# Batch 0 of a cosine attention with a low-rank mixer: keys transposed unnormed, their norms in the scale of the exp

## The chip, the cores and the metric

One NeuronCore of a Trainium2 chip runs the whole program. The metric is the time of one execution in device microseconds (us). Its engines work side by side and wait for each other through semaphores: TensorE (PE in the profile), VectorE (DVE), ScalarE (ACT), GpSimd (POOL) and SyncE (SP), the last two used here mainly to issue transfers. Each engine takes its instructions in the order in which the program lists them.

## What is computed

For 8 batches, 12 heads, 448 positions and 64 dimensions, cosine attention and then a mixer whose weights all batches share (d_model 768, rank 32, hidden 3072):

```python
q_n = q / (norm(q) + 1e-06);  k_n = k / (norm(k) + 1e-06)
scores = q_n @ k_n.T / tau                     # tau = 0.1
attn = softmax(scores)
x = (attn @ v) as [batch, seq, heads * dim]
u = x + (x.T @ U @ V).T
out = u + relu(u @ w_ch1) @ w_ch2
```

The scores are cosines divided by tau, so the kernel leaves the maximum of the softmax out and divides by the sum of the exps after the product with v.

## The kernel before

**Data.** q, k, v and the weights come from HBM in float32 and are cast to bfloat16 by the transfers themselves, which GpSimd issues (`load_qk`, `load_v0`, `load_v`, `load_w1`, `load_w2`). U and V come through SyncE as float32 and are cast by ScalarE (`cast_u`, `cast_v`). A position of the sequence is stored as s = 4 * row + c, so a tile of q or k has 112 rows and, per head, 4 chunks c of 64 dimensions.

**Norms** (`stats`). For a group of two or four heads, q and k are squared (L434 on ScalarE, L436 on VectorE), summed over the dimensions (L440, VectorE), and the inverse norm comes from Ln and Exp on ScalarE (L445, L448), then an addition of epsilon and a reciprocal on VectorE (L451, L453). It lands in a tile `inv`.

**Normed heads** (`norm`, pairs of heads). Two multiplies for the keys (L477) and one for the queries (L474) fill a tile `xn` of twelve blocks of 128 columns. Blocks 0 to 7 are keys: the first four hold head 0 in columns 0 to 63, the others head 1 in columns 64 to 127, and the other halves are zeros set once (L705). Blocks 8 to 11 hold the queries of both heads beside each other. For batches 0 and 1, `flip` transposes the blocks on TensorE (L363) against an identity, eight key blocks into one PSUM tile and four query blocks into another, and copies them to `qkT` (L700 on ScalarE, L702 on VectorE). Later batches use the transposing transfer.

**Attention** (`attention`). Per pair of batch 0 eight score matmuls (L508) of 112 key rows against 448 queries contract over all 128 rows, of which one half is zero; ScalarE takes the exp of each (L512) with the scale 1/tau. Then 16 matmuls per head multiply with v (L526), the sum of the exps coming along as an extra column of ones, and VectorE divides (L533, L535). The `attn` tiles are two, the PSUM tiles of scores three, the `qk_nat` tiles of loaded q and k three.

**v of batch 0** (`load_v0`). It is loaded in the order of q and k in two transfers (L408) and copied by ScalarE or VectorE into a layout with two extra columns, both lying in the space that w2 takes later.

**Mixer** (`stage0`, `mlp`). The products with U (L559) and V (L587), the addition of x (L601, and L596, L598 where two batches meet), transposes of u, then per batch 24 groups of six up-projection matmuls (L649) with a relu each (L659, L661), and the down-projection (L670) with the addition of u (L679). Two batches share seven row tiles: the even batch takes three, the odd one four.

**What sets the order.** Nothing is scheduled by hand. Every operation is put into a `Plan` with an engine (or two to choose from), a cost, its dependencies, the buffers that it takes and frees, and a priority (a low number goes first). `Plan.run` plays the program through with these costs and writes each engine's instructions down in the order of their planned starts. The chip keeps that order on each engine, whatever the times turn out to be. TensorE has several streams in a fixed precedence: transposes of q and k, products with v, the mixer's first matmuls, scores, and last the projections. Transfers on GpSimd have a planned busy time on one shared line (0.5 us per head for each of q and k, and for v of batch 0) and a planned delay (2 us, for later batches 8 us).

Of the kernel before, what the change touches and what calls it, by code (L numbers as in the profile page):

```python
# [200 lines left out]
def kernel(  # L201
# [45 lines left out]
    def fixed_ring(tiles):  # L247
# [10 lines left out]
    r_ln = ring(2, [SCH, 2, G, SC], FP, "ln")  # L258
    r_inv = ring(3, [SCH, 2, G, SC], FP, "inv")
    r_qkT = ring(6, [128, 12, SCH], BF, "qkT")  # L260
# [5 lines left out]

    VN = H * SC * D
    r_w2 = Ring(1, lambda i: pool.tile([128, VN + H * SC * (D + 2)], BF, name="raw_v", tag="w2", bufs=1)
                if i == 0 else pool.tile([128, NC, C], BF, name="w2_sb", tag="w2", bufs=1))
# [4 lines left out]

    def v_raw():
        return raw.tile[0:SCH, 0:VN].rearrange("p (h e) -> p h e", h=H)

    def v_first():
        return raw.tile[0:SCH, VN:].rearrange("p (h c d) -> p h c d", h=H, c=SC)

# [14 lines left out]
    V_sb = const.tile([128, PAD + S + PAD], BF, name="V_sb")  # L295
    ident = const.tile([128, 128], BF, name="ident")
    w1_sb = const.tile([128, CC, F], BF, name="w1_sb")

# [14 lines left out]
    plan = Plan()  # L313
    pe_tp = plan.stream("PE")
    pe_av = plan.stream("PE")
    pe_a = plan.stream("PE")
# [37 lines left out]

    def flip(stream, ins, n, into, part, deps, acq, rel):

        tp = Slot(r_mm, 1)
        tp.own = True
        for z, x in enumerate(ins):
            def fn(z=z, x=x):  # L360
                if z == 0:
                    tp.tile = psum.tile([128, len(ins), n], BF, name="tp", tag="mm", bufs=3)
                nc.tensor.transpose(out=tp.tile[:, z, :], in_=x(), identity=ident[:n, :n])  # L363
            o = plan.add(Op("PE", 0.05, fn, deps=deps + [id_set] if z == 0 else (), acq=[tp] + acq,
                            rel=rel if z == len(ins) - 1 else []), stream)
        c = plan.add(Op("ACT/DVE", any_t(n * len(ins), 2), None, deps=[o], acq=acq, rel=[tp],
                        prio=0.2, fast=True))
        c.fn = lambda: copy_op(c, *part(into(), tp.tile))
        return c
# [4 lines left out]

    def load_qk(b, h0, h1):
        ld = Slot(r_ld, 3 * (h1 - h0) // 2)
        ops = [load(lambda i=i, src=src: nc.gpsimd.dma_start(  # L377
            out=ld.tile[:, i, 0:h1 - h0, :],
            in_=src[b, h0:h1].rearrange("h (s c) d -> s h (c d)", c=SC)),
            (h1 - h0) * 0.5, acq=[ld], late=2.0 if b == 0 else LATE) for i, src in enumerate((q, k))]  # L380
        return ld, ops

# [23 lines left out]
    def load_v0(h0, h1):  # L406

        o = load(lambda: nc.gpsimd.dma_start(  # L408
            out=v_raw()[:, h0:h1, :], in_=v[0, h0:h1].rearrange("h (s c) d -> s h (c d)", c=SC)),
            (h1 - h0) * 0.5, acq=[raw])  # L410
        c = plan.add(Op("ACT/DVE", any_t(256 * (h1 - h0), 2), None, deps=[o, v0_set], prio=0.35,
                        fast=True))
        c.fn = lambda: copy_op(c, v_first()[:, h0:h1, :, 0:D],
                               v_raw()[:, h0:h1, :].rearrange("p h (c d) -> p h c d", c=SC))
        for h in range(h0, h1):
            got[0, h, "v"] = [c]

    def stats(b, h0, h1, ld, ops):

        g = h1 - h0  # L420
        pr = 0.3 if b == 0 else 4
        ss, ln, nv, inv = Slot(r_ss, 1), Slot(r_ln, 1), Slot(r_ln, 1), Slot(r_inv, 3 * g // 2)
        red = []
        for i in range(2):
            for a0 in range(0, g, G // 2):
                a1 = min(g, a0 + G // 2)
                sq = Slot(r_sq, 1)
                o = Op("ACT/DVE" if b == 0 else "DVE", any_t(256 * (a1 - a0), 2, 0.17), None,
                       deps=[ops[i]], acq=[sq], prio=pr + 0.2, fast=True)

                def square(o=o, i=i, a0=a0, a1=a1, sq=sq):
                    x, y = ld.tile[:, i, a0:a1, :], sq.tile[:, 0:a1 - a0, :]
                    if o.by == "ACT":
                        nc.scalar.activation(out=y, in_=x, func=AF.Square)  # L434
                    else:
                        nc.vector.tensor_mul(y, x, x)  # L436
                o.fn = square
                plan.add(o)
                red.append(plan.add(Op("DVE", dve_t(256 * (a1 - a0)),
                    lambda i=i, a0=a0, a1=a1, sq=sq: nc.vector.reduce_sum(  # L440
                        ss.tile[:, i, a0:a1, :].rearrange("p h c -> p (h c)"),
                        sq.tile[:, 0:a1 - a0, :].rearrange("p h (c d) -> p (h c) d", d=D),
                        axis=AX.X),
                    deps=[o], acq=[ss], rel=[sq], prio=pr + 0.1)))
        o = plan.add(Op("ACT", 0.25, lambda: nc.scalar.activation(  # L445
            ln.tile[:, :, 0:g, :], ss.tile[:, :, 0:g, :], AF.Ln),
            deps=red, acq=[ln], rel=[ss], prio=0))
        o = plan.add(Op("ACT", 0.2, lambda: nc.scalar.activation(  # L448
            nv.tile[:, :, 0:g, :], ln.tile[:, :, 0:g, :], AF.Exp, scale=0.5),
            deps=[o], acq=[nv], rel=[ln], prio=0))  # L450
        o = plan.add(Op("DVE", 0.21, lambda: nc.vector.tensor_scalar_add(  # L451
            nv.tile[:, :, 0:g, :], nv.tile[:, :, 0:g, :], EPS), deps=[o], prio=pr))
        o = plan.add(Op("DVE", 0.35, lambda: nc.vector.reciprocal(  # L453
            inv.tile[:, :, 0:g, :], nv.tile[:, :, 0:g, :]), deps=[o], acq=[inv], rel=[nv], prio=pr))
        for p in range(h0 // 2, h1 // 2):
            norm(b, p, ld, inv, 2 * p - h0, [o], pr)

    count = [0]

    def norm(b, p, ld, inv, a, deps, pr):  # L460


        by_pe = b < PE_BATCHES
        xn, qkT = Slot(r_xn, 2 if by_pe else 1), Slot(r_qkT, 8 if b == 0 else 7)
        deps = deps + [xn_set[count[0] % len(xn_t)]]
# [30 lines left out]
    def attention(b, p, X):  # L496
        off = PAD * (b % 2)
        qkT, qdeps = got.pop((b, p, "qkT"))
        attn = Slot(r_attn, 2)
        exps = {}  # L500
        small = b == 0
        rows_ = SCH if small else 128
        for m in range(8 if small else 7):
            sc = Slot(r_sc, 1)

            def score(sc=sc, m=m):
                kT = qkT.tile[:, 0:8, :].rearrange("p b s -> p (b s)")
                nc.tensor.matmul(out=sc.tile[0:rows_, 0:S], lhsT=kT[:, rows_ * m:rows_ * (m + 1)],  # L508
                                 rhs=qkT.tile[:, 8:12, :].rearrange("p c s -> p (c s)"),
                                 start=True, stop=True)  # L510
            o = plan.add(Op("PE", pe_t(S), score, deps=qdeps, acq=[sc], rel=[qkT]), pe_sc)
            exps[m] = plan.add(Op("ACT", act_t(S), lambda sc=sc, m=m: nc.scalar.activation(  # L512
                out=attn.tile[0:rows_, m, off:off + S], in_=sc.tile[0:rows_, 0:S], func=AF.Exp,
                scale=inv_tau), deps=[o], acq=[attn], rel=[sc], prio=0.1 if b == 0 else 1))
        muls = []
# [182 lines left out]
    def copy_op(op, dst, src):  # L698
        if op.by == "ACT":
            nc.scalar.copy(out=dst, in_=src)  # L700
        else:
            nc.vector.tensor_copy(out=dst, in_=src)  # L702


    xn_set = [fill(lambda t_=t_: nc.vector.memset(t_[:, 0:8, :], 0.0), 1024, prio=i - 3)  # L705
              for i, t_ in enumerate(xn_t)]
# [19 lines left out]
    def load_u(par):  # L726
        off = PAD * par
        ops = []
        for t in range(4):
            lo, hi = max(0, 128 * t - off), min(S, 128 * (t + 1) - off)  # L730
            for n, c, s0, s1 in segments(lo, hi):
                r0 = n + off - 128 * t
                ops.append(plan.add(Op("SP", 0.45, lambda t=t, c=c, s0=s0, s1=s1, r0=r0: nc.sync.dma_start(  # L733
                    out=U_f()[r0:r0 + s1 - s0, par, t, :], in_=rows(moe_U, c, s0, s1)),
                    deps=[zf], prio=-2, lat=2.5)))
        return ops
# [4 lines left out]
    def cast_v():  # L741
        nc.scalar.copy(out=V_sb[:, PAD:PAD + S].rearrange("r (c s) -> r s c", c=SC),
                       in_=V_f().rearrange("r (s c) -> r s c", c=SC))

# [10 lines left out]
    def att(b):  # L755
        X = Slot(r_X, 0)
        muls = []
        for p in range(NPAIR):
            muls += attention(b, p, X)
        return stage0(b, X, muls)  # L760

    u0 = load_u(0)
    v0 = [plan.add(Op("SP", 0.45, lambda t=t: nc.sync.dma_start(out=V_f()[R * t:R * (t + 1)], in_=moe_V),  # L763
                      acq=[uv], prio=-2, lat=2.5)) for t in range(4)]
    u1 = load_u(1)
    first = load_qk(0, 0, 2)
    id_set = plan.add(Op("POOL", 0.5, lambda: make_identity(nc, ident)), pool_q)
    stats(0, 0, 2, *first)
    go(0, 2, 4)
    load_v0(0, 4)  # L770
    go(0, 4, 8)
    load_v0(4, 12)
    go(0, 8, 12)
    for i in range(NW):
        w1_ops.append(load_w1(i, NW))
    consts = [plan.add(Op("ACT", 0.25, lambda: cast_u(0), deps=u0 + [z], rel=[uv], prio=3)),
              plan.add(Op("ACT", 0.5, cast_v, deps=v0 + [z], rel=[uv], prio=3)),
              plan.add(Op("ACT", 0.25, lambda: cast_u(1), deps=u1 + [z], rel=[uv], prio=3))]
# [55 lines left out]
```

## Time and profile before

| what | us |
|---|---|
| median of the runs (3, 611.57 to 612.37) | 612.14 |
| the profiled execution's own time | 612.43 |
| span from its first to its last instruction | 610.5 |
| TensorE busy | 585.5 |
| VectorE busy | 298.6 |
| ScalarE busy | 285.0 |
| first score of batch 0 starts | 16.02 |
| first exp of batch 0 starts | 16.59 |
| last exp of batch 0 ends | 44.92 |
| first up-projection of batch 0 starts | 48.05 |
| first transposes of batch 1 start | 61.05 |
| first down-projection of batch 0 starts | 89.65 |

Times inside the execution count from the start of the span. Busy time counts an instruction from its start to its end; TensorE's matmuls are pipelined and their ends are modelled, so a busy TensorE is not one at its peak. A row of a timeline gives start, duration, engine, line, operation, output and input, and, in brackets, how long the engine stood idle before it and what it waited for. The chain of waits is followed back from the last instruction: at each step to what released it, or to the instruction before it on its engine.

### The profile page before, as it was taken

What the parts mean: (1) busy time and instruction counts of PE and PEld (TensorE: products, weight loads), DVE (VectorE), ACT (ScalarE), POOL (GpSimd) and SP (SyncE); (2) the same over time, 40 slices, a digit from 0 to 9 for tenths busy, and PEclk for the clock granted to TensorE, in tenths of its full rate; (3) what the DMA queues carried; (4) which work ended last, traced back from release to release, by engine and by line L of the source; (5) the groups of instructions that cost most, each with busy time, mean ns of one, the idle gap of its engine ahead of it and who ended that gap; (6) DMA issues with size and microseconds to landing.
All of it is one profiled execution on the core that took longest, in us unless ns stands there. A gap on an engine that the chain in (4) does not pass through costs nothing.

```text
span 610.5 us, 11561 instructions
## 1 busy us (share of the span) xinstructions
PE 585.5 (96%) x4704; PEld 348.3 (57%) x4728; DVE 298.6 (49%) x758; ACT 285.0 (47%) x609; POOL 109.9 (18%) x168
## 2 busy tenths in 40 slices
PE   0899999999999999999999999999999999999997
PEld 0565666555555665666445666666545666654465
DVE  6977859989999799654820253014300210110011
ACT  4984981288774187407642067505542015014300
POOL 6227160135340627000600000000000000000000
PEclk9999999999999999999999999999999999999999
DMA  9999992999999999644962132031002110410011
GB/s 136 202 204 136 210 156 23 166 138 138 132 125 155 139 185 159 94 84 83 121 37 53 53 72 59 1 84 35 14 1 52 52 40 1 79 52 1 0 53 53
DMA packets 146037, 54.58 MB, mean 89 GB/s; under 512 B 109568, under 2 KB 145984, under 8 KB 145984
## 3 DMA queue, kind: packets, MB, share of 16 engines
q0 software_dynamic: 69216, 25.96, 37.9%
q1 hardware_dynamic: 76704, 27.86, 24.5%
q8 instruction: 37, 0.61, 0.4%
q14 instruction: 16, 0.13, 0.1%
q10 hardware_dynamic: 64, 0.02, 0.0%
HBM read 52.25 MB, written 11.01 MB: 104 GB/s over the span
## 4 chain that ended last, share of the span: by engine, by line
PE 91%; ACT 4%; DVE 2%; SPq 1%; DMA 1%; issue 1%; ACTq 0%
PE mm L670 36%; PE mm L649 35%; PE sc L508 9%; PE av L526 7%; ACT attn L512 3%; PE mm L587 1%; DMA raw_uv<-in_moe_U_dram 1%; PE tp L363 1%; SPq L733 1%; PE mm L559 1%; DVE ss L440 1%; ACT qkT L700 0%; ACT sq L434 0%; ACT uT L700 0%; SPq L763 0%
## 5 line engine op out<-in xcount | busy, mean ns | idle before, releaser
L649 PE MATMUL mm<-uT,w_sb 128*128 128x384 bf16 (+1 forms) x1130 | 235.4, 352 | 0.9
L670 PE MATMUL mm<-w_sb,relu 128*128 128x384 bf16 (+1 forms) x1368 | 233.7, 323 | 0.3 <-ACT uT L700 0.3
L512 ACT ACTIVATE attn<-sc 128x448 bf16<-128x448 f32 (+1 forms) x342 | 165.1, 557 | 91.4 <-PE av L526 57.6
L670 PEld LDWEIGHTS <-relu 128*128 128x128 bf16 x1368 | 132.5, 98 | 87.1 <-issue 1.3
L649 PEld LDWEIGHTS <-w_sb 128*128 128x128 bf16 x1152 | 112.2, 98 | 101.1 <-issue 0.2
L659 ACT ACTIVATE relu<-mm 128x384 bf16<-128x384 f32 (+1 forms) x174 | 95.0, 546 | 150.4 <-PE mm L649 148.6
L679 DVE TENSOR_TENSOR O_sb<-mm,u_nat 128x384 f32<-128x384 f32 (+1 forms) x57 | 31.1, 549 | 231.1 <-PE mm L670 227.6
L508 PE MATMUL sc<-qkT 128*128 128x448 bf16 (+1 forms) x342 | 103.5, 359 | 7.8 <-DVE qkT L702 4.1
L526 PEld LDWEIGHTS <-attn 128*128 128x128 bf16 (+1 forms) x1536 | 61.1, 98 | 16.1 <-issue 2.2
L399 POOL DMA_DIRECT2D v_nat<-in_v_dram x98 | 63.3, 651 | 21.2 <-DMA w_sb<-in_moe_w_ch_dram 5.3
L440 DVE TENSOR_REDUCE ss<-sq 112x8 f32<-112x512 bf16 x96 | 62.9, 672 | 0.5 <-ACT sq L434 0.3
L526 PE MATMUL av<-v_nat,attn 128*128 128x65 bf16 x1344 | 55.6, 193 | 0.0
L377 POOL DMA_DIRECT2D qk_nat<-in_q_dram x25 | 17.8, 713 | 172.3 <-DVE xn L474 115.9
L508 PEld LDWEIGHTS <-qkT 128*128 128x128 bf16 (+1 forms) x342 | 31.3, 104 | 26.0 <-issue 5.8
L535 DVE TENSOR_TENSOR X_sb<-av,rd 128x256 bf16<-128x256 f32 x96 | 40.2, 419 | 1.6
L477 DVE TENSOR_TENSOR xn<-qk_nat,inv 112x256 bf16<-112x256 bf16 x96 | 36.8, 415 | 1.9 <-DMA qkT<-xn 1.8
L533 DVE RECIPROCAL rd<-av 128x4 f32<-128x4 f32 x96 | 17.0, 179 | 34.7 <-PE av L526 33.6
L436 DVE TENSOR_TENSOR sq<-qk_nat 112x512 bf16<-112x512 bf16 x85 | 32.8, 412 | 0.0
L474 DVE TENSOR_TENSOR xn<-qk_nat,inv 112x512 bf16<-112x512 bf16 x48 | 32.6, 680 | 0.0
L601 DVE TENSOR_TENSOR u_nat<-mm,X_sb 128x384 bf16<-128x384 f32 (+2 forms) x45 | 22.4, 527 | 12.7 <-PE mm L587 12.0
L363 PE MATMUL tp<-ident,xn 112*128 112x112 bf16 x144 | 11.2, 226 | 10.4 <-DVE xn L477 10.4
L445 ACT ACTIVATE ln<-ss 112x32 f32<-112x32 f32 (+1 forms) x25 | 6.2, 248 | 31.9 <-DVE ss L440 31.9
(51 smaller groups left out, 175.4 us busy)
## 6 DMA issues: line engine op xcount, KB each, us to landing
qk_nat<-in_q_dram POOLq DMA_DIRECT2D x23, 224.0 KB, 5.7
qk_nat<-in_k_dram POOLq DMA_DIRECT2D x23, 224.0 KB, 6.8
w_sb<-in_moe_w_ch_dram POOLq DMA_DIRECT2D x4, 1152.0 KB, 18.7
w_sb<-in_moe_w_ch_dram POOLq DMA_DIRECT2D x8, 576.0 KB, 14.1
out_dram<-O_sb SPq DMA_DIRECT2D x15, 168.0 KB, 2.2
out_dram<-O_sb SPq DMA_DIRECT2D x16, 144.0 KB, 2.1
out_dram<-O_sb SPq DMA_DIRECT2D x16, 120.0 KB, 1.9
out_dram<-O_sb SPq DMA_DIRECT2D x16, 96.0 KB, 2.2
```

Of the source, the lines that this page charges most:

```text
L399: nc.gpsimd.dma_start(out=vb[p0:p0 + s1 - s0, hs, j, 0:D], in_=v[b, hs].rearrange("h (s c) d -> c s h d", c=SC)[c, s0:s1]),
L436: nc.vector.tensor_mul(y, x, x)
L440: lambda i=i, a0=a0, a1=a1, sq=sq: nc.vector.reduce_sum(ss.tile[:, i, a0:a1, :].rearrange("p h c -> p (h c)"), sq.tile[:, 0:a1 - a0, :].re ...
L474: nc.vector.tensor_mul(dst, src, sc.to_broadcast([SCH, 2, SC, D]))
L477: nc.vector.tensor_mul(dst, src[:, hh], sc[:, hh].to_broadcast([SCH, SC, D]))
L508: nc.tensor.matmul(out=sc.tile[0:rows_, 0:S], lhsT=kT[:, rows_ * m:rows_ * (m + 1)], rhs=qkT.tile[:, 8:12, :].rearrange("p c s -> p (c s)" ...
L512: exps[m] = plan.add(Op("ACT", act_t(S), lambda sc=sc, m=m: nc.scalar.activation(out=attn.tile[0:rows_, m, off:off + S], in_=sc.tile[0:row ...
L526: nc.tensor.matmul(out=av.tile[:, t, 0:D + 1], lhsT=attn.tile[0:rows_, m, 128 * t:128 * (t + 1)], rhs=vv[0:rows_, h, j, 0:D + 1], start=(j ...
L535: muls.append(plan.add(Op("DVE", dve_t(256), lambda av=av, rd=rd, h=h: nc.vector.tensor_mul(X.tile[:, :, h * D:(h + 1) * D], av.tile[:, :, ...
L649: o = plan.add(Op("PE", pe_t(n), lambda f=f, cc=cc, mm=mm: nc.tensor.matmul(out=mm.tile[:, 0:n], lhsT=w1_sb[:, cc, f * 128:(f + 1) * 128], ...
L659: nc.scalar.activation(out=relu.tile[:, f, 0:n], in_=mm.tile[:, 0:n], func=AF.Relu)
L670: nc.tensor.matmul(out=mm.tile[:, 0:c1 - c0], lhsT=relu.tile[:, f, i * 128:(i + 1) * 128], rhs=w2.tile[:, f, c0:c1], start=(f == 0), stop= ...
```

## The change

All of it concerns batch 0 and the start.

- The loaded keys are transposed as they are, 64 columns at a time: four chunks of head 0 into partitions 0 to 63 and of head 1 into 64 to 127 of one PSUM tile with four blocks, where there were eight. They wait for the load alone. The keys' two multiplies vanish, the queries keep theirs.
- The keys' inverse norm, with tau multiplied in at the epsilon step (a new small tile `taus`), is read by the exp as its scale, one number per partition.
- A score matmul contracts over 64 rows, the lower half of the array for head 0, the upper for head 1. It has a TensorE stream of its own, `pe_first`, next after the transposes.
- Each third of v is loaded in four transfers, one per chunk, straight into the layout with the extra columns, behind the q and k of the third after it. The copies vanish.
- Heads 0 to 3 share one tile of loaded q and k, so all of batch 0 takes three.
- The squares of heads 4 to 11 and the qkT copies of all pairs but the first go to VectorE only.
- The casts of U and V are planned 12 us behind their transfers' issue in place of 2.5, V's loop order is turned round, and the memsets of `xn` go last.

```diff
-    r_inv = ring(3, [SCH, 2, G, SC], FP, "inv")
+    r_inv = ring(4, [SCH, 2, G, SC], FP, "inv")
...
+    taus = const.tile([SCH, 2, G * SC], FP, name="taus")
...
     pe_tp = plan.stream("PE")
+    pe_first = plan.stream("PE")
     pe_av = plan.stream("PE")
...
-                nc.tensor.transpose(out=tp.tile[:, z, :], in_=x(), identity=ident[:n, :n])
+                m = 128 // wide
+                nc.tensor.transpose(out=tp.tile[m * (z % wide):m * (z % wide + 1), z // wide, :], in_=x(),
+                                    identity=ident[:n, :n])
...
-        o = load(lambda: nc.gpsimd.dma_start(
-            out=v_raw()[:, h0:h1, :], in_=v[0, h0:h1].rearrange("h (s c) d -> s h (c d)", c=SC)),
-            (h1 - h0) * 0.5, acq=[raw])
-        c = plan.add(Op("ACT/DVE", any_t(256 * (h1 - h0), 2), None, deps=[o, v0_set], prio=0.35,
-                        fast=True))
...
+        ops = [load(lambda c=c: nc.gpsimd.dma_start(
+            out=v_first()[:, h0:h1, c, 0:D],
+            in_=v[0, h0:h1].rearrange("h (s c) d -> c s h d", c=SC)[c]),
+            (h1 - h0) * 0.22, deps=[v0_set], acq=[raw]) for c in range(SC)]
...
-                o = Op("ACT/DVE" if b == 0 else "DVE", any_t(256 * (a1 - a0), 2, 0.17), None,
+                o = Op("ACT/DVE" if b == 0 and h0 < 4 else "DVE", any_t(256 * (a1 - a0), 2, 0.17), None,
...
+                nc.vector.scalar_tensor_tensor(out=n, in0=n, scalar=EPS, in1=taus[:, :, 0:g * SC],
+                                               op0=ALU.add, op1=ALU.mult)
...
+    def norm_q(p, ld, ops, la, inv, a, o, pr):
+        xn, qkT = Slot(r_xn, 1), Slot(r_qkT, 8)
+        EV = "DVE" if p else "ACT/DVE"
+        done = [flip(pe_tp, [(lambda c=c, hh=hh: ld.tile[:, 1, la + hh, c * D:(c + 1) * D])
+                             for c in range(SC) for hh in range(2)],
+                     SCH, lambda: qkT.tile, (lambda t_, x: (t_[:, 0:4, :], x)), [ops[1]], [qkT], [ld], 2, EV)]
+        def unit():
+            src = ld.tile[:, 0, la:la + 2, :].rearrange("p h (c d) -> p h c d", d=D)
+            nc.vector.tensor_mul(
+                xn.tile[:, 8:12, :].rearrange("p c (h d) -> p h c d", h=2), src,
+                inv.tile[:, 0, a:a + 2, :].unsqueeze(3).to_broadcast([SCH, 2, SC, D]))
...
+                dims = slice(D * (m // 4), D * (m // 4 + 1)) if small else slice(0, 128)
+                nc.tensor.matmul(out=sc.tile[0:rows_, 0:S], lhsT=kT[dims],
+                                 rhs=qkT.tile[dims, 8:12, :].rearrange("p c s -> p (c s)"),
...
+                    scale = inv.tile[:, 1, a + m // 4, m % 4:m % 4 + 1]
...
-    xn_set = [fill(lambda t_=t_: nc.vector.memset(t_[:, 0:8, :], 0.0), 1024, prio=i - 3)
+    xn_set = [fill(lambda t_=t_: nc.vector.memset(t_[:, 0:8, :], 0.0), 1024, prio=8)
...
-        nc.scalar.copy(out=V_sb[:, PAD:PAD + S].rearrange("r (c s) -> r s c", c=SC),
-                       in_=V_f().rearrange("r (s c) -> r s c", c=SC))
+        nc.scalar.copy(out=V_sb[:, PAD:PAD + S].rearrange("r (c s) -> r c s", c=SC),
+                       in_=V_f().rearrange("r (s c) -> r c s", c=SC))
...
-                      acq=[uv], prio=-2, lat=2.5)) for t in range(4)]
+                      acq=[uv], prio=-2, lat=12.0)) for t in range(4)]
...
-    go(0, 2, 4)
+    stats(0, 2, 4, *load_qk(0, 2, 4, first[0], 2))
+    go(0, 4, 8)
     load_v0(0, 4)
-    go(0, 4, 8)
-    load_v0(4, 12)
     go(0, 8, 12)
+    load_v0(4, 8)
+    load_v0(8, 12)
...
-              plan.add(Op("ACT", 0.5, cast_v, deps=v0 + [z], rel=[uv], prio=3)),
+              plan.add(Op("ACT", 1.0, cast_v, deps=v0 + [z], rel=[uv], prio=3)),
```

## The prediction

> **What bounds the kernel now.** I read the clock row first (1.000 throughout, so no stage is throttled), then the busy shares by stage, then the waits of TensorE, then the chain of the stages with idle time.
>
> ```profile
> core 0: us, PE busy (x) PEld busy (x) DVE busy (x) ACT busy (x) POOL busy (x), PEclk, DMA share, GB/s
> 0.00:16.02 16.02, 1.48 (x12) 1.15 (x13) 10.60 (x34) 8.37 (x15) 10.52 (x20) 1.00 1.11 139
> 16.02:48.05 32.03, 28.14 (x338) 18.86 (x339) 26.38 (x70) 28.57 (x66) 9.02 (x14) 1.00 1.26 202
> 48.05:60.89 12.84, 12.84 (x80) 7.74 (x81) 9.27 (x23) 6.24 (x14) 10.96 (x16) 1.00 1.21 128
> ...
> 119.73:600.00 480.27, 478.60 (x3644) 277.95 (x3665) 203.21 (x508) 210.06 (x444) 64.75 (x98) 1.00 0.52 74
> 600.00:610.50 10.50, 6.96 (x67) 5.56 (x65) 1.27 (x3) 0.00 (x0) 0.00 (x0) 1.00 0.20 58
> ```
>
> The first two columns are a stretch and its length, the third is TensorE. From 48.05, where the first up-projection matmul runs (L649), TensorE is full: 555.8 of 562.5 us, and 3.5 of the missing 6.6 are the tail. So the end moves with the start of batch 0's up-projection, T0 = 48.05, as long as no new hole opens behind it. Ahead of T0 TensorE works 29.6 us and idles 18.4, most of it in two waits:
>
> ```profile
> PE tp L363 <- DVE xn L477: 10.4, 1, 10.4
> PE sc L508 <- DVE qkT L702: 4.1, 1, 4.1
> ```
>
> The second is explained by the ScalarE and VectorE rows in order of time:
>
> ```profile
> 11.39 2.18 ACT L742 CAST V_sb<-raw_uv 128x448 bf16<-128x448 f32 x1 [1.73 <-DMA raw_uv<-in_moe_V_dram]
> 13.08 0.51 ACT L445 ACTIVATE ln<-ss 112x16 f32<-112x16 f32 x1
> 13.15 1.29 ACT L700 COPY raw_v<-raw_v 112x1024 bf16<-112x1024 bf16 x1
> 14.34 0.21 ACT L448 ACTIVATE ln<-ln 112x16 f32<-112x16 f32 x1
> ```
> ```profile
> 14.58 0.34 DVE L451 TENSOR_SCALAR ln<-ln 112x16 f32<-112x16 f32 x1 [3.29 <-ACT ln L448]
> 14.95 0.25 DVE L453 RECIPROCAL inv<-ln 112x16 f32<-112x16 f32 x1
> 15.12 0.85 DVE L702 COPY qkT<-tp 128x896 bf16<-128x896 bf16 x2
> ```
>
> ScalarE waits for V's transfer, casts V, copies v, and only then gives the norms of heads 2 and 3. VectorE waits for those, and the copy that pair 0's scores need stands behind that wait. After 16 us the chain is ScalarE alone up to 37 us:
>
> ```profile
> 26.48 0.52 ACT sq L434
> 27.00 1.30 ACT attn L512 x3
> 28.30 0.52 ACT sq L434
> 28.82 1.30 ACT attn L512 x3
> ...
> 30.50 2.17 ACT attn L512 x5
> ```
>
> An exp in a row of exps takes 0.435 us (2.17 / 5), a square 0.52.
>
> **The change, step by step.**
>
> *To the first exp (16.59 now).* The two reduces of pair 0 run 7.08 to 8.4, as now. The memsets ahead of them keep their number, xn's three (0.48 each) only trade places within VectorE's wait for data; the new tau memsets have a 112x96 row of 0.14 as bound. Ln, exp, eps and reciprocal end at 9.45. I add one key copy of 0.38 (128x448 row) that may stand in between: 9.83. The query multiply follows at once (0.68; the two key multiplies, 0.75, are gone): 10.5. Four transposes take 0.6 with their latency, then the copy 0.38 and the 0.62 that now lie between copy end and exp start: first exp at 12.1, which is 4.5 earlier. The key transposes need only the load (landed at about 6) and are beside this. The casts of U and V get a due time 12 us behind their issue, in place of 2.5, so they no longer stand ahead of the norms; their data lands by 15.2 in either order. The v copies (1.29 on ScalarE, 0.68 on VectorE) vanish.
>
> *From first to last exp of batch 0 (16.59 to 44.92, 28.3 us, ScalarE busy 27.1).* Out: five squares that become VectorE's, 5 x 0.52 = 2.6; four qkT copies, 4 x 0.42 = 1.7. In: the casts of U, 2 x 0.30, and of V. V's loop order changes, which no row shows: at most today's 2.18, at least the 0.30 of 128x128; I take 0.70, the row of a 128x512 cast, nearest in elements. So 28.3 - 4.3 + 1.3 = 25.3. Then the exps read their scale from a column of `inv` in place of a number. No ACTIVATE of the trace has such an operand. It fetches one more element per partition, so below is nothing (the exp row itself), and above a whole ACTIVATE of 16 columns, 0.21. I take 0.05, nearer the exp row because only the operand differs: 48 x 0.05 = 2.4, so 27.7. Last exp ends at 39.8, and with the 3.13 us from there to T0 unchanged, T0' = 42.95, 5.1 earlier.
>
> [...]
>
> *VectorE in that stage* is busy 23.5 of 28.3. Out: ten key multiplies (0.375 each in a pair's 0.75) 3.8, the v copy 0.7, narrower key copies 6 x 0.23 = 1.4. In: the squares 5 x 0.38, four copies 4 x 0.38. That leaves 21.0 of 27.7: beside ScalarE, priced at nothing. Were that cover gone, a bubble per pair of heads would cost about 1 us.
>
> *TensorE.* As many transposes and scores as before; the scores stream the same 448 columns through half the rows. Saved or lost: between half the 48 x 0.19 us (both halves side by side; the order 0 to 3, then 4 to 7 forbids most of it) and up to 0.23 us, the row of a transpose, at each change between shapes. I take nothing: TensorE has 3.9 us idle in this stage and ScalarE sets the pace.
>
> *GpSimd and the transfers.* Twelve v transfers replace two. At 0.65 us (L399) they issue in 7.8 us, but the last q and k no longer wait 4.34 us for a buffer: w1 issues from about 15.2 in place of 13.25. Small rows move slowly: 68 GB/s in a stretch with v alone (51.6 to 53.3) against 206, so v's 0.69 MB may take 10 us in place of 3.4, and everything behind it comes 2 to 6.5 us later. w1's quarters landed from 24 to 41.5; the last is wanted at T0' + 17.5 = 60. w2 landed from 60.4 to 80; the first eighth is wanted at about 74. Both hidden; all the later v transfers have v's own 2 us or more before their pair's turn.
>
> *Behind T0', a hole.* The order of each engine is fixed from planned due times. Planned transfer time for batch 0's v rises from 12 x 0.5 to 12 x 4 x 0.22 us, by 4.6, and batch 1's q, k and v and w2 become due that much later, while the up-projection is due about 5 earlier. Now batch 1's first transposes come after 80 of the 144 up-projection matmuls (13.00 us). 9.6 us more at 0.1625 are 59 more: 139 of 144. So the filler that batch 1's first two pairs enjoy now is used up. From there TensorE holds their work alone: 36 transposes (0.6 per twelve) and 14 scores (0.19 each), 4.5 us, until w2's and v's due times let the down-projection in. The chain is 2.0 (61.05 to 63.04, transposes to first score) and 14 exps of 0.435, 8.1 in all. Hole: 8.1 - 4.5 = 3.6 us; bounds 0 (matmuls of the first layer are left among them) and 8 (nothing overlaps). After that the first layer of batch 1 has 72 down-projection matmuls as cover (107.60 to 119.73), enough.
>
> **Sum.** 612.43 is the profiled execution's own time (span 610.5 and 1.9 around it); - 5.1 + 3.6 = 610.9. That execution is 0.3 above the median 612.14, so 610.6 against the runs.
>
> **Rivals.**
> 1. *The scale operand is dear and ScalarE gives everything back* (the slower side). Place: 48 exps on the one engine that the chain runs through. T0' = 40.55 + 48p, the time 608.5 + 48p on the profiled execution's base, so the gain is gone at p = 0.081 us and turns round from there; at the upper bound 0.21 it is 618.6. For it: ScalarE has no slack. Against: the fetch may hide behind the exp before. At half the bound, 0.105, it is 613.2 against the runs, the value I give it.
> 2. *The hole is larger*: batch 1 comes late and everything waits, 8 us: 615.0. For it: the filler really is short. Against: its data lands at 43 to 49, well before its due time.
> 3. *No hole*: the order keeps first-layer matmuls beside batch 1, as now: 607.0; with a free operand 604.6. Against: the due times above.
> 4. *The halves do not do what they say*: scores no shorter. True in my sum already, costing nothing.
>
> **Chances.** Forecast 0.40 (three quarters of it faster by over 0.2%, about what a measurement of this kernel can tell from no change, the rest within), rival 1 0.27 (0.19 slower, 0.08 within), rival 2 0.13 (0.12 slower, 0.01 within), rival 3 0.20 (faster). Faster 0.50, within 0.19, slower 0.31. The range leaves out a free operand without any hole and an operand above 0.15 us: 606.3 to 615.5; the forecast's own, operand from nothing to 0.08, is 608.2 to 612.1.
>
> **What would show it.** First exp near 12 and no wait of VectorE for an Ln before it: step one. Exps in a row at 0.435 or 0.53: the operand. ScalarE unbroken and VectorE with gaps up to 40 us: step two. TensorE idle just after the up-projection of batch 0, with batch 1's first transposes behind matmul 139 or so: the hole. Wrong would be: VectorE or a v transfer ending the waits of scores, or up-projection matmuls waiting for w1.

## The result and the profile after

The changed kernel takes 628.21 us (median of 4 runs, 626.02 to 628.67), the kernel before 612.22 beside it (4 runs, 611.57 to 612.37): a ratio of 1.0256, 95% interval 1.0231 to 1.0281. It is 2.6% slower, 16.0 us by the medians. The profiled execution took 628.38 with a span of 626.5.

The stages of the kernel after, with the columns of the first fence of the prediction (start and end, length, TensorE busy, its weight loads, VectorE, ScalarE, GpSimd, clock row, share of the transfer engines, GB/s):

```profile
0.00:16.00 16.00, 5.15 (x39) 2.76 (x39) 13.85 (x43) 8.06 (x16) 13.16 (x25) 1.00 1.20 130
16.00:48.00 32.00, 32.00 (x225) 16.39 (x224) 15.47 (x43) 23.38 (x45) 11.48 (x16) 1.00 1.25 191
48.00:61.00 13.00, 12.21 (x94) 7.26 (x94) 7.37 (x22) 4.91 (x9) 11.56 (x17) 1.00 1.32 120
...
120.00:600.00 480.00, 478.52 (x3702) 277.33 (x3700) 222.45 (x560) 215.58 (x459) 65.99 (x100) 1.00 0.54 76
```

Read the second row against the one of before (28.14 us for 338 matmuls). TensorE is now busy for all 32.00 us of the stage, for 225 matmuls, and ScalarE, which had little slack before (28.57 of 32.03 us busy), is busy for 23.38. A full TensorE looks good in a table; here it got less done. The last row has TensorE as full as before (478.52 of 480.00 us, 478.60 of 480.27 before), so most of the loss lies ahead of 120 us.

The reason is in the duration of single rows. TensorE in the kernel after, in order of time (start, duration, engine, line, operation):

```profile
12.16 1.28 PE L537 MATMUL sc<-qkT 64*112 64x448 bf16 x3
...
25.90 3.44 PE L537 MATMUL sc<-qkT 64*112 64x448 bf16 x7
...
36.35 1.06 PE L562 MATMUL av<-raw_v,attn 112*128 112x65 bf16 x16
...
59.68 22.90 PE L685 MATMUL mm<-uT,w_sb 128*128 128x384 bf16 x129
82.42 0.56 PE L363 MATMUL tp<-ident,xn 112*128 112x112 bf16 x8
```

And in the kernel before:

```profile
16.02 1.28 PE L508 MATMUL sc<-qkT 128*112 128x448 bf16 x3 [4.12 <-DVE qkT L702]
...
22.45 0.79 PE L508 MATMUL sc<-qkT 128*112 128x448 bf16 x3
...
24.62 0.67 PE L526 MATMUL av<-raw_v,attn 112*128 112x65 bf16 x16
...
48.05 13.16 PE L649 MATMUL mm<-uT,w_sb 128*128 128x384 bf16 x80
61.05 0.56 PE L363 MATMUL tp<-ident,xn 112*128 112x112 bf16 x8
```

A single matmul's duration holds its latency (0.62 us for a score of the kernel after, where scores without a wait start 0.37 apart), so the pace comes from a row of several: the duration, less that of the first, over the number of steps. Before 21 us both kernels take 0.37 us per score. From about 21.5 us the kernel before takes 0.19 to 0.23 (two scores start 0.188 apart at 43.07, those of the row at 22.45 start 0.21 and 0.23 apart), while the kernel after keeps 0.47 in this row of seven and 0.37 where scores follow without a wait (1.37 for three, first one 0.62), up to its last score near 52 us. The product with v is the same instruction in both, on 112 rows, and its 16 take 1.06 in place of 0.67. So everything on TensorE runs at half pace through batch 0's attention and for a while behind it, also what the diff does not touch. The up-projection starts at 59.68 in place of 48.05, 11.6 later, and even its first twelve matmuls start 0.32 apart, up to 63.2 us; from there on it is 0.162, as in the kernel before.

The clock row does not tell it: it shows 1.00 in all these stages. The trace shows why. Its record of the clock begins only where the pace doubles, at 63.28 us in the kernel after and at 21.80 in the kernel before, and ahead of its first entry the row reads 1.00.

ScalarE's exps, as a group of the page (instruction and count, busy time and mean ns of one, idle time ahead of them and its cause):

```profile
L546 ACT ACTIVATE attn<-sc,inv 112x448 bf16<-112x448 f32 x48 | 28.3, 634 | 11.3 <-PE sc L537 11.3
```

Two things stand in it: an exp is longer (634 ns on average, 588 in the kernel before), and ScalarE now waits 11.3 us for scores. In the prediction it was to wait for nothing.

### The profile page after: what moved, and what is told of

Read it like the earlier page. It is cut to its first block, busy times and chain, and to the rows that moved or that the text cites. A ratio compares the mean times of both kernels' runs of the same rounds, so it can differ in the third digit from the quotient of the medians.

```text
span 626.5 us, 11581 instructions
## 1 busy us (share of the span) xinstructions
PE 608.1 (97%) x4728; PEld 354.9 (57%) x4728; DVE 294.2 (47%) x754; ACT 286.3 (46%) x601; POOL 116.5 (19%) x178
## 4 chain that ended last, share of the span: by engine, by line
PE 94%; DVE 4%; ACT 1%; issue 0%; ACTq 0%
PE mm L685 35%; PE mm L706 34%; PE sc L537 12%; PE av L562 9%; PE tp L363 2%; PE mm L623 1%; ACT attn L546 1%; PE mm L595 1%; DVE u_nat L637 1%; DVE ss L439 0%; DVE O_sb L715 0%; DVE xn L741 0%; ACT qkT L736 0%; DVE xn L505 0%; DVE u_nat L634 0%
## 5 line engine op out<-in xcount | busy, mean ns | idle before, releaser
L706 PE MATMUL mm<-w_sb,relu 128*128 128x384 bf16 (+1 forms) x1368 | 238.3, 323 | 0.2 <-DVE O_sb L715 0.2
L685 PE MATMUL mm<-uT,w_sb 128*128 128x512 bf16 (+1 forms) x1152 | 234.9, 354 | 0.0
L546 ACT ACTIVATE attn<-sc 128x448 bf16<-128x448 f32 x294 | 140.9, 550 | 80.7 <-PE av L562 51.5
L537 PE MATMUL sc<-qkT 128*128 128x448 bf16 (+1 forms) x342 | 111.8, 386 | 1.4 <-ACT attn L546 0.3
L562 PEld LDWEIGHTS <-attn 128*128 128x128 bf16 (+1 forms) x1536 | 64.3, 101 | 25.1 <-issue 8.1
L435 DVE TENSOR_TENSOR sq<-qk_nat 112x512 bf16<-112x512 bf16 x92 | 35.5, 411 | 0.0
L546 ACT ACTIVATE attn<-sc,inv 112x448 bf16<-112x448 f32 x48 | 28.3, 634 | 11.3 <-PE sc L537 11.3
L505 DVE TENSOR_TENSOR xn<-qk_nat,inv 112x256 bf16<-112x256 bf16 x84 | 32.3, 411 | 2.2 <-DMA qkT<-xn 2.1
L502 DVE TENSOR_TENSOR xn<-qk_nat,inv 112x512 bf16<-112x512 bf16 x42 | 28.7, 682 | 0.0
L379 POOL DMA_DIRECT2D qk_nat<-in_k_dram x25 | 17.5, 702 | 3.4 <-PE tp L363 2.9
```

The lines of the kernel that those rows point to most:

```text
L379: ops = [load(lambda i=i, src=src: nc.gpsimd.dma_start(out=ld.tile[:, i, lo:lo + h1 - h0, :], in_=src[b, h0:h1].rearrange("h (s c) d -> s ...
L505: nc.vector.tensor_mul(dst, src[:, hh], sc[:, hh].to_broadcast([SCH, SC, D]))
L537: nc.tensor.matmul(out=sc.tile[0:rows_, 0:S], lhsT=kT[dims], rhs=qkT.tile[dims, 8:12, :].rearrange("p c s -> p (c s)"), start=True, stop=True)
L546: nc.scalar.activation(out=attn.tile[0:rows_, m, off:off + S], in_=sc.tile[0:rows_, 0:S], func=AF.Exp, scale=scale)
L562: nc.tensor.matmul(out=av.tile[:, t, 0:D + 1], lhsT=attn.tile[0:rows_, m, 128 * t:128 * (t + 1)], rhs=vv[0:rows_, h, j, 0:D + 1], start=(j ...
L685: o = plan.add(Op("PE", pe_t(n), lambda f=f, cc=cc, mm=mm: nc.tensor.matmul(out=mm.tile[:, 0:n], lhsT=w1_sb[:, cc, f * 128:(f + 1) * 128], ...
```

## The experiments

**Theory P, the pace:** a score that uses 64 of the 128 rows of the array does not count, or counts too little, as work that brings TensorE to its full pace; nothing else of the change is needed. **Rivals:** the scale operand makes the exps so dear that the rest follows; the early transposes of the keys or the other order hold the pace down; or TensorE was never warmed up and would keep its pace once it had it. Times in us; T0 is the start of batch 0's first up-projection in the profiled execution. The plan is played anew for every kernel. In e1, e3, e10 and, against e4, e7 the instructions of VectorE, ScalarE and GpSimd stay on their engines and in their order; in the other runs the plan moved or added some. Each ratio is to the kernel before as run beside it (medians 612.22 to 612.32).

| run | median (range) | ratio to before, interval | T0 |
|---|---|---|---|
| before | 612.22 (611.57 to 612.37) | 1 | 48.05 |
| after | 628.21 (626.02 to 628.67) | 1.0256 (1.0231 to 1.0281) | 59.68 |
| e1 before, half rows | 623.77 (622.24 to 625.50) | 1.0185 (1.0159 to 1.0212) | 58.01 |
| e2 after, full rows | 614.03 (613.09 to 614.85) | 1.0027 (1.0016 to 1.0037) | 46.36 |
| e3 after, warm-up | 627.43 (625.92 to 627.54) | 1.0239 (1.0223 to 1.0254) | 58.08 |
| e4 before, late casts | 610.03 (609.88 to 610.75) | 0.9963 (0.9948 to 0.9977) | 45.83 |
| e5 before, scale operand | 616.62 (616.52 to 617.19) | 1.0074 (1.0060 to 1.0087) | 52.37 |
| e6 e4 and v straight | 611.75 (611.31 to 612.66) | 0.9993 (0.9984 to 1.0002) | 46.33 |
| e7 e4 and warm-up | 609.71 (609.47 to 610.41) | 0.9961 (0.9948 to 0.9973) | 45.56 |
| e8 after, side by side | 616.34 (615.40 to 616.84) | 1.0065 (1.0052 to 1.0079) | 48.31 |
| e9 e2 and a number as scale | 611.29 (610.87 to 612.37) | 0.9987 (0.9978 to 0.9995) | 43.98 |
| e10 after, a number as scale | 628.25 (626.86 to 628.35) | 1.0255 (1.0241 to 1.0269) | 58.72 |

**e1: the half rows alone.** The kernel before, its keys still normed and transposed as they were; only the score leaves out the half of the rows that is zero.

```diff
-    nc.tensor.matmul(out=sc.tile[0:rows_, 0:S], lhsT=kT[:, rows_ * m:rows_ * (m + 1)],
-                     rhs=qkT.tile[:, 8:12, :]...
+    dims = slice(D * (m // 4), D * (m // 4 + 1)) if small else slice(0, 128)
+    nc.tensor.matmul(out=sc.tile[0:rows_, 0:S], lhsT=kT[dims, rows_ * m:rows_ * (m + 1)],
+                     rhs=qkT.tile[dims, 8:12, :]...
```

> The kernel before with one thing of the change alone: batch 0's score matmuls contract over the 64 rows that hold keys, in place of 128 rows of which half are zeros. Theory P (half-array scores hold TensorE at half pace): scores of batch 0 stay at 0.37 us each as at the very start, where before they fall to 0.19 from about 21.5 us on; the first up-projection comes 4 to 10 us later than 48.05 and itself starts at half pace; the time is 617 to 626. Theory Q (the half rows are free, the pace is lost through the new order, the half-width transposes or the exp's scale): scores at 0.19 from 21.5 us on, T0 at 48, the time 611 to 613.

Measured: 623.77, 11.5 more than before. TensorE in order of time:

```profile
28.79 2.21 PE L509 MATMUL sc<-qkT 64*112 64x448 bf16 x5
...
58.01 6.18 PE L650 MATMUL mm<-uT,w_sb 128*128 128x384 bf16 x37
```

Five scores in 2.21 is 0.40 apiece behind the first, where the kernel before has 0.19. The record of the clock begins at 53.03, in place of 21.80. One edit, which removes nothing but rows of zeros and reorders no other instruction, moves T0 by 10.0. That is theory P by itself; no operand, transpose, transfer or order is needed for it.

**e2: everything but the half rows.** The kernel after, its scores over all 128 rows again. The other halves of the key blocks are zeros that GpSimd writes, and one more copy per pair puts the two heads into place.

```diff
+            nc.gpsimd.memset(t_[64:128, 0:4, :], 0.0)
+            nc.gpsimd.memset(t_[0:64, 4:8, :], 0.0)
+            copy_op(c, t_[0:64, 0:4, :], tp.tile[0:64])
+            copy_op(c, t_[64:128, 4:8, :], tp.tile[64:128])
...
-                dims = slice(D * (m // 4), D * (m // 4 + 1)) if small else slice(0, 128)
+                dims = slice(0, 128)
```

> The changed kernel with the score matmuls of batch 0 contracting over 128 rows again: the transposed keys of each head are copied into blocks of their own and GpSimd zeroes the other halves, which costs 12 memsets on GpSimd and one copy more per pair. Order and everything else as changed. Theory P: scores at 0.19 us from about 20 us on, the first up-projection at 42 to 47 instead of 59.7, the time 607 to 614. Theory Q: nothing gained, 626 to 630.

Measured: 614.03. Of the 16.0 us, 14.2 come back, although zeros are multiplied in place of nothing. So it is the rows that take part, not the data in them. The change remains 0.3% slower than before (interval 0.16 to 0.37%), and the rest of the study goes for that remainder. A part of it is once more the pace. The stage from 48 to 61 us (columns as above), and TensorE's up-projection:

```profile
48.00:61.00 13.00, 13.00 (x77) 7.59 (x76) 4.74 (x11) 6.02 (x13) 10.23 (x16) 0.94 1.33 114
```
```profile
46.36 22.75 PE L691 MATMUL mm<-uT,w_sb 128*128 128x384 bf16 x129
```

In this execution, the slowest of the eight, the trace has the clock at 0.50 from 46.23 to 49.65, with full rows everywhere. The first eleven up-projection matmuls start 0.32 apart, which costs some 1.6 us behind T0; in e9 the same 129 take 21.13.

**e3: full pace to begin with.** The kernel after, with 45 matmuls of the identity over the whole array ahead of the first score, whose result is not used.

```diff
+                for _ in range(45):
+                    nc.tensor.matmul(out=wt.tile[:, 0:128], lhsT=ident, rhs=ident, start=True, stop=True)
```

> The changed kernel with 45 full-array matmuls of the identity against itself between the first key transposes and the first query transposes, where TensorE waits anyway. Their result is not used. Theory P with the pace held open only by work on the full array: the dummies reach 0.06 us each, the first scores too are at 0.19, but the pace falls back within some microseconds and the time stays above 620. Theory P with the pace merely needing to be opened once: scores at 0.19 to the end of batch 0, T0 at 43 to 47, the time 608 to 614. Theory Q: no matmul changes its pace, 626 to 630.

Measured: 627.43, no gain that counts. TensorE in order of time, then the stages (columns as above):

```profile
11.97 0.72 PE L547 MATMUL sc<-qkT 64*112 64x448 bf16 x3 [0.30 <-ACT qkT L746]
...
24.31 3.45 PE L547 MATMUL sc<-qkT 64*112 64x448 bf16 x7
```
```profile
16.00:48.00 32.00, 32.00 (x228) 16.50 (x229) 15.77 (x43) 23.14 (x45) 11.08 (x16) 0.50 1.25 193
48.00:61.00 13.00, 12.21 (x89) 7.23 (x87) 8.54 (x24) 4.56 (x9) 11.83 (x18) 0.53 1.32 121
```

The first three half-row scores do run at full pace (0.72 for three, 0.19 apiece behind the first), so half a row count is not slow as such. Near 16 us, about 6 us after the warm-up, the pace falls back and stays down, with TensorE busy without a gap (32.00 of 32.00). And here the clock row does say it: 0.50. It is the same stage with the same work as in the kernel after, whose row says 1.00. In both the matmuls take the same time (1.37 us for three scores in a row, at 21.06 in the kernel after and at 19.47 here), so the 1.00 of the kernel after was not the clock that it ran at. This rules out the rival that TensorE only has to be warmed up. The fall by itself is not proof against half rows, for in e7, with full rows, the pace falls some 8 us after a warm-up too; but there it is back after 3.41 us, and here it stays down up to 60.16.

The 45 matmuls of the warm-up take 4.07 us, from 6.03, and the first scores behind them have the full pace. Busy time alone does not keep it: TensorE was busy for 32.00 of 32.00 us and stayed at 0.50. The events of the clock that the traces hold fall where the pace changes (63.28 in the kernel after, 15.79 and 60.16 in e3); what misleads is the row ahead of the first one.

**e4: the late casts alone.** The kernel before with the due times of the casts of U and V and V's loop order as in the change.

```diff
...
-                      acq=[uv], prio=-2, lat=2.5)) for t in range(4)]
+                      acq=[uv], prio=-2, lat=12.0)) for t in range(4)]
...
```

> The kernel before with the casts of U and V alone moved: planned 12 us behind their transfers, V's loop order turned round, planned cost 1.0. This takes the wait away that held VectorE 3.29 us. All theories: first exp 3 to 4 us earlier, at about 13; if ScalarE sets the pace from there, T0 at 44 to 45.5 and the time 608 to 609.5; if the later stages take it back, 610 to 612.

Measured: 610.03, 2.3 less than before, and faster than both kernels. The first score starts at 12.90 in place of 16.02, T0 is 45.83, and batch 1's first transposes stand at 57.53 with 72 up-projection matmuls ahead of them. So of the 3.1 us won at the start 2.2 reach T0, and nothing is given back behind it. (The plan also gives two of the five squares between first and last exp to VectorE.)

**e5: the scale operand.** The kernel before, the exps of batch 0 reading 1/tau from a column in place of taking it as a number.

```diff
-                scale=inv_tau), deps=[o], acq...
+                scale=col[0:rows_, 0:1] if small else inv_tau), deps=[o, col_set], acq...
```

> The kernel before with one thing of the change alone: the exps of batch 0 read their scale from a column (all 1/tau, so the same numbers) in place of a number. Theory 'dear operand' (0.09 us each, as the changed kernel's exps in a row suggest): exps in a row at 0.525 instead of 0.435, ScalarE's stage 4.3 us longer, T0 at 51 to 52.4, the time 615 to 616.5. Theory 'hidden operand': the difference in a row comes from waits for scores, T0 within 0.7 of 48.05, 611.5 to 613.

Measured: 616.62, 4.3 more; T0 52.37, also 4.3 more. ScalarE in order of time:

```profile
16.83 1.68 ACT L513 ACTIVATE attn<-sc,col 112x448 bf16<-112x448 f32 x3 [0.62 <-PE sc L509]
```

Three exps in 1.68 where the kernel before has 1.30 to 1.41: 0.09 apiece (exps in a row come 0.525 apart against 0.435). 48 x 0.09 = 4.3, and ScalarE sets the pace there, so the sum reaches the end. That the two agree to a tenth is partly luck: with the column's memset in it the plan also takes three squares from ScalarE between first and last exp (1.6 us) and gives it one more copy of qkT and wider ones (1.1 us). The mechanism of rival 1 of the prediction is real and its price is 0.09.

**e6: late casts, and v straight into place.** e4 with v's twelve transfers and their place behind q and k, and no copies.

```diff
...
+        ops = [load(lambda c=c: nc.gpsimd.dma_start(
+            out=v_first()[:, h0:h1, c, 0:D],
+            in_=v[0, h0:h1].rearrange("h (s c) d -> c s h d", c=SC)[c]),
+            (h1 - h0) * 0.22, deps=[v0_set], acq=[raw]) for c in range(SC)]
...
```

> The kernel before with the late casts and with batch 0's v loaded straight into place in twelve transfers, in the order of the changed kernel. If the copies of v were on the path of ScalarE: 1 us less ahead of the first exp than with the late casts alone, which would be 608.5 to 609.5 against 610.0. If the small rows and the longer issue on GpSimd hold batch 1 or w2 up, or the planned due times move batch 1 back and open a hole: 611 to 613.

Measured: 611.75, 1.7 above e4. T0 moves only 0.5, to 46.33. The rest is behind it: batch 1's first transposes go from 57.53 to 62.42, behind 99 up-projection matmuls in place of 72. This fits the prediction's last step, in which the longer planned transfers make batch 1 later; the copies that they save were not on the path.

**e7: late casts and a warm-up.** e4 with 85 identity matmuls from 3.38 to 10.31, unused.

> The kernel before with the late casts and with 85 full-array matmuls of the identity against itself, their result unused, in the first wait of TensorE (3.5 to 10.4 us). If the half pace of the first 9 us of batch 0 costs something: scores at 0.19 from the first, T0 0.5 to 1.5 earlier than 45.83, 608.5 to 609.5. If ScalarE sets the pace there: no change, 609.7 to 610.5.

Measured: 609.71, not to be told from e4 (the intervals of the ratios lie on each other). The first scores take 0.19 apiece from 12.66 to about 17, where the kernel before is at 0.37 until 21, and T0 moves by 0.3. Then the pace falls (the trace has the clock at 0.50 from 17.88 to 21.29), so the run tries the faster TensorE for some 5 us of batch 0. There, beside full rows and a ScalarE that sets the pace, it is worth nothing that the runs can tell: the prediction's "ScalarE sets the pace" holds at both paces in these first microseconds, as long as the rows are full.

**e8: both halves at the same time.** The kernel after, each score of head 0 followed at once by that of head 1 into another PSUM tile, so that the halves of the array can work beside each other.

```diff
+                o.fn = lambda sc=sc, sc2=sc2, m=m, one=score: (one(sc, m), one(sc2, m + 4))
```

> The changed kernel with the two heads' score matmuls of the same key block issued back to back, one on the lower and one on the upper half of the array, into two PSUM tiles (one of them of the ring that transposes use). Theory P: if the halves run at the same time they count as a full array, the pace rises and the time falls to 611 to 619; if they run one after the other, or if a half counts for nothing either way, the pace stays and the time is 622 to 630. Scores' cost side by side: eight in 4 x 0.37 at half pace.

Measured: 616.34, 11.9 less than after. TensorE in order of time:

```profile
22.56 0.62 PE L537 MATMUL sc<-qkT 64*112 64x448 bf16 x1
22.57 0.62 PE L537 MATMUL mm<-qkT 64*112 64x448 bf16 x1
```

The two start 0.01 us apart and run together, which the order 0 to 3, then 4 to 7 of the kernel after forbids but where 3 meets 4 (0.004 apart at 14.37). The pace is still half at 22.6 and rises at 31.28; it is half again from 38.10 to 44.93 and from 48.34 to 51.76, the start of the up-projection. So pairs do better than single halves (628.21) and worse than full rows (614.03). The order of the scores and one PSUM tile changed with them, so this suggests that the share of the array in use matters, and does not show where the limit is.

**e9 and e10: a number as scale.** e2, and the kernel after, with one eighth of 1/tau as a number in place of the operand. Both leave the norms of the keys out of the scores.

```diff
-                    scale = inv.tile[:, 1, a + m // 4, m % 4:m % 4 + 1]
+                    scale = inv_tau * 0.125
```

> The kernel after with its batch 0 scores over all 128 rows (as in e2, 614.03) and with a number, one eighth of 1/tau, as the scale of batch 0's exps in place of the column of inv; the keys' own norms are left out of the result by this. All waits and the order of the instructions stay. If the operand costs 0.09 on each of 48 exps and ScalarE sets the pace once the rows are full, 4.3 us go: T0 from 46.4 to 42 to 43, the whole 609.5 to 610.5, less if the hole behind T0 takes part of it back (batch 1's start is tied to the number of up-projection matmuls ahead of it, so it moves with T0). Rival: something else of the change than rows and operand (late loads of v, one stream more, the fixed order) holds the rest of e2's loss, and it stays above 613.

> The kernel after with a number, one eighth of 1/tau, as the scale of batch 0's exps in place of the column of inv, and nothing else; the keys' own norms are left out of the result. The scores stay on half the rows. If TensorE at 0.37 us per score and half pace sets the end of batch 0's attention, the exps are not what it waits for, and the 4.3 us that the operand costs beside full rows shrink to a part: 626 to 628 (after: 628.2), T0 58.5 to 59.7. Rival: the two costs add whatever the pace, then 624.

Measured: e9 611.29, 2.7 less than e2; e10 628.25, the 628.21 of the kernel after. The operand costs 4.3 in the kernel before, 2.7 beside full rows in the changed order (e2's fall of the pace at T0 included), and nothing that the runs can tell beside half rows. The two costs do not add: in these runs whichever engine sets the pace hides the other's. ScalarE in e2 and in e9, in order of time:

```profile
27.42 14.26 ACT L552 ACTIVATE attn<-sc,inv 112x448 bf16<-112x448 f32 x27
```
```profile
26.83 12.26 ACT L552 ACTIVATE attn<-sc 112x448 bf16<-112x448 f32 x27
```

Both run 27 exps without a gap that counts, 0.53 and 0.45 apiece. In e10 there is no such row; behind its first eight, the exps come in rows of four at most, mostly singly or in twos and behind a wait for a score.

e9 also sizes the hole behind T0. Its T0 is 43.98, 4.1 before that of the kernel before, and its span only 1.4 shorter (609.1 against 610.5), so 2.6 us are given back. Here are all of TensorE's matmuls, and then those on the tiles `w_sb`, the mixer's large weights, in the 15 us that follow batch 1's first transposes (64.94 and 61.05), first in e9:

```profile
65.00:80.00 15.00, 13.69 (x161) 1.00 1.16 210
```
```profile
65.00:80.00 15.00, 6.02 (x27) 1.00 1.16 210
```

And in the kernel before:

```profile
61.00:76.00 15.00, 14.40 (x160) 1.00 1.16 210
```
```profile
61.00:76.00 15.00, 8.84 (x41) 1.00 1.16 210
```

There are 14 projections fewer, so the filler has run short, but as many matmuls in all, and TensorE idles for 1.31 in place of 0.60. So these rows show 0.7 of the 2.6 us as idle time; where the rest goes was not taken apart. In e9, as in e2 and the kernel after, 129 up-projection matmuls come ahead of batch 1's first transposes, in the kernel before 80.

## Why the prediction was wrong

It gave 610.6 with a range to 615.5; the time is 628.2. One step failed by more than the whole range.

**The step that failed: TensorE.** "I take nothing: TensorE has 3.9 us idle in this stage and ScalarE sets the pace." The bounds beside it, half of 48 x 0.19 saved to 0.23 per change of shape lost, were all about single scores. What was at stake was the pace of everything. In the kernel before that pace is not constant: scores take 0.37 until about 21 us and 0.19 from then on, and the very fence that I read of the stage from 16 to 48 was an average over both. At half pace TensorE's work no longer fits beside ScalarE: 48 x 0.19 = 9 us more for the scores, and twelve times 0.4, some 5 us, for the products with v, against 3.9 idle. The cover was worked out at full pace, and the edit took the pace away. By T0 the half rows cost 13.3 us (59.68 in place of e2's 46.36). The shift of the pace was in the trace of before, near 21.8 us; that it hung on the number of rows was not, and it took e1 to show it. What it costs if the cover is gone was priced for VectorE (about 1 us per pair of heads) and never for TensorE: it would have been the 9 and the 5.

**Rival 4 had the place and no price.** "The halves do not do what they say" was put down as costing nothing. A rival that is priced at nothing has not been thought through to its worst case; this one cost 11.5 alone (e1) and 14.2 within the change (e2).

**The clock row.** "1.000 throughout, so no stage is throttled" was a wrong reading already of the kernel before: its scores up to 21 us have half the later pace under the same 1.000, and its record of the clock begins only at 21.80.

**First exp: right in kind, 0.6 late.** Predicted 12.1, measured 12.73. VectorE no longer waits for the casts; but the inverse norms end at 10.20 in place of 9.45, since it runs the reduces of the next group too (four in a row, 7.14 to 9.83) ahead of the epsilon step, for which ScalarE was ready at 9.22. What follows takes 2.5, about as predicted. The late casts alone, 2.3 us (e4), are the best part of the change.

**ScalarE's stage: the operand was under-sized.** I took 0.05, rival 1 turned at 0.081, measured is 0.09. With it and full rows, the prediction's own formula gives T0 = 40.55 + 48 x 0.09 = 44.9; e2 has 46.36. With a free operand 40.55; e9 has 43.98. Of those 3.4 us, 0.6 are the first exp, 1.0 the exps (12.74 to 39.1, 26.4 in place of 25.3), and 1.8 lie between the last exp and T0, which took 3.13 before and 4.9 in e9; why that grew I did not try. V's cast took 0.98, not 0.70.

**The hole: right in kind, 1.0 us too large.** Predicted were 139 of 144 up-projection matmuls ahead of batch 1's first transposes and 3.6 us lost. Measured are 129 in the kernel after, in e2 and in e9, and by T0 and span 2.6 us given back in e9. In e2 and the kernel after it is 4.3, of which 1.6 and 1.8 go to the first up-projection matmuls at half pace. In e6 it shows by itself and smaller, with 99 matmuls and 1.0 us.

**Transfers: hidden, as said.** w1 was issued from 17.35 in place of the 15.2 expected, and no up-projection matmul waited for it; what v's transfers cost came through the planned order (e6), not through late data.

**The sum, mended.** From e9, which has neither cost, 611.3: the operand adds 2.7 (e2, with its fall of the pace at T0), the half rows 14.2 (after). The gain of the change without them, some 1 us, is less than half of what the late casts give alone.

## What to carry to other kernels

Read the pace of an engine from rows of several equal instructions in different stages of the trace, not from a clock row or from its busy share: an engine that is 100% busy may be doing half of what it could (TensorE from 16 to 48 us in the kernel after and in e3). Before a matmul is cut to fewer rows because the others are zero, ask what the rows of zeros do beside computing; leaving them out was 11.5 us dearer than multiplying them (e1). Where an edit is costed at nothing because an engine has slack, work that slack out again at the engine's slower pace.

Of the versions run, the kernel before with nothing but the late casts (e4, 610.03; with a warm-up e7, 609.71, not to be told from it) beats both kernels.

## What the runs showed of the hardware

- Scores on 64 of TensorE's 128 rows kept it at half pace although it was busy without a gap (32.00 of 32.00 us at 0.50 in e3). That rows count is shown by e1 and e2, which differ from their base in nothing else that touches TensorE's scores; how they are counted, and where the limit is, was not measured. Products with v on 112 rows and transposes were among that work and did not bring the pace up. Nor does the pace return with the last half-row score: that ends at 52.36 in the kernel after and at 50.77 in e3, and the clock rises at 63.28 and 60.16. In e1 it rises at 53.03, ahead of the last one, which starts at 53.69.
- Full rows can lose the pace too. It fell for 3.41 us in e2 (from 46.23), e5 (from 30.99) and e7 (from 17.88), each time behind 3.41 us of which TensorE was busy for 2.32, 1.74 and 1.71. In e3, with half-row scores, it fell behind 3.41 us with 2.71 busy. The clock's recorded changes lie 3.41 us or a multiple of it apart (e8: 31.28, 38.10, 44.93, 48.34, 51.76).
- The clock row can show 1.00 at half pace: in the kernels before and after, while the same work has 0.50 in e3, where the pace had risen once before. In all three the row reads 1.00 up to the first entry of the trace's record.
- Two half-row matmuls on different halves, issued one behind the other, start 0.01 us apart (e8).
- A scale read from a column costs an exp of 448 elements 0.09 us, also in a row of exps (e5).
